# Attention gathered into the first batch's MoE, the other batches' MoE in two phases, and a fast product for two of them

## The chip, the cores and the metric

The kernel runs on one core of a Trainium2 chip. The core has a matmul engine (TensorE, PE in the rows), three engines for elementwise work (VectorE = DVE, ScalarE = ACT, GpSimd = POOL), and SyncE (SP), on whose queue this kernel issues all its transfers. PSUM is split into eight banks of 512 floats for each of 128 partitions; matmuls write there, and GpSimd does not read it. The metric is device time of one execution in microseconds (us). Three runs of the kernel before took 859.25, 853.92 and 858.77 us, median 858.77. The profile is that of one execution, with a span of 857.7 us from the first to the last instruction.

## What is computed

Four batches of attention (8 heads, 576 positions, 64 per head), then two feed-forward layers over all 2304 tokens. The attention of a head is the sum of two: a coarse one over means of four positions, repeated back to 576, and a local one in which a position sees only those less than four away.

```python
out_d = sm_attn(q_d, k_d, v_d)               # 144 x 144 per head
out_up = np.repeat(out_d, factor, axis=2)
mask = np.abs(pos[:, None] - pos[None, :]) < factor
...
x = (out_up + out_local).transpose(0, 2, 1, 3).reshape(B * S, H * D)   # 2304 x 512
h = x @ moe_w_in                             # 512 -> 2048
g = h * np.clip(h + 3.0, 0.0, 6.0) / 6.0
x = g @ moe_w_out                            # 2048 -> 512
h = np.maximum(np.maximum(x @ w1, x @ w2), x @ w3)   # 512 -> 768, three times
out = h @ moe2_w_out                         # 768 -> 512
```

q, k and v are float32; the weights of both layers arrive as float64, and the kernel makes float32 of them itself.

## The kernel before

**Products.** A float32 operand x is split into two float16 parts, hi and lo, scaled by a power of two, and a product is three float16 matmuls: hi hi, hi lo and lo hi. Each such matmul is one instruction of 128 x 128 weights on 288 (first MoE), 384 or 512 columns (second MoE). The scales come from `pow2_scale`, a chain of some ten small operations that begins with sums of squares.

**First MoE.** A batch has 576 tokens in two halves of 288. For each half and each of the 16 blocks f of 128 hidden units, `moe1_h` makes h in a bank (12 matmuls, L1052), ACT makes Relu of h (r, L1063), DVE the product with h (gf, L1067), ACT the hi part of g (L1070), DVE or POOL the lo part (L1072), and `moe1_y` multiplies g with the weights of `wo` into four accumulators y (12 matmuls, L1086). h and y alternate: the h of later blocks stands between an h and its y. Batch 0 goes through the weights in four quarters, as they arrive, and adds y to the sum of the quarters on DVE (L1113) or POOL (L1110); batches 1 to 3 keep the accumulators over all 16 blocks.

**Weights.** `quarter` loads a quarter of w_in and w_out as 64-bit words, `to_f32` makes float32 of them in four passes, two on POOL (L899, L902) and two on DVE (L905, L909: the last sets the sign), ACT sums squares (L949), and `split` in L1005 and L1007 makes hi and lo. The weights of the second layer are loaded and converted in the same way by `m2_load` and `m2_wo`, during batch 3's MoE and the first pass of MoE 2.

**Attention** of a batch: loads of k, q, v (`load`, tile stg) and of a second layout of v (`load_vw`, 8 transfers per half); `transposes` into kT and qT (L581, L593) with sums of four positions (qkd, L614); `local_scores` (L756) and its softmax `soft`; `down_scores` (L657), one unit (two heads, one half of the positions) at a time; `down_pT` (L700), `down_out` (L717), `local_out` (L822), which adds both into x (L834), and `x_split` (L491, L493) into the fp16 pair x16. Most of its tiles have one buffer per name, so a batch's attention follows the one before. Batch 0's attention comes first; that of batch b > 0 is spread over the MoE of batch b - 1 and the first part of its own MoE.

**Second MoE.** Three passes over 768 tokens. w1, w2 and w3 each multiply y by seven products of half-size blocks where eight would be needed (`m2_a`, L1417; sums of blocks stand for the eighth), DVE takes the maximum over the three, and `m2_out` multiplies with w_out (L1488). `y_ops` makes the seven token operands, `m2_w1` and `m2_w23` the seven weight operands.

**Order.** All this is given as operations with a cost and a priority to `Plan`, which lays them out on the engines by list scheduling when the kernel is built; `PARAMS` holds the priorities and some choices (which sums go to POOL, which masks to PE). The instruction streams are then fixed: each engine goes through its own in order. PSUM banks have tags: at 2 (attention, output), h 2, y 4. A tile's buffers are given out in the order of the operations, tag `at` in any order. Where PE would stand idle before 94 us of the plan's time, `warm_up` matmuls that compute nothing are put in.

## Time and profile before

| | |
|---|---|
| median of three runs | 858.77 us (853.92 to 859.25) |
| span of the profiled execution | 857.7 us, 20,891 instructions |
| PE busy | 806.4 us, 94% |
| DVE busy | 564.2 us, 66% |
| ACT busy | 408.4 us, 48% |
| POOL busy | 201.7 us, 24% |
| HBM read and written | 49.8 and 4.7 MB |

The profiled execution's span is 1.1 us below the median. Matmuls overlap, so PE's busy time counts the stretches in which any runs, and says nothing of how much each does. The granted clock of PE is given as a share of 2.4 GHz; its two levels are 1.2 and 2.4, and a value between is a mean over the stretch.

### The profile page before, as it was taken

What the parts mean: (1) busy time and instruction counts of PE and PEld (TensorE: products, weight loads), DVE (VectorE), ACT (ScalarE), POOL (GpSimd) and SP (SyncE); (2) the same over time, 40 slices, a digit from 0 to 9 for tenths busy, and PEclk for the clock granted to TensorE, in tenths of its full rate; (3) what the DMA queues carried; (4) which work ended last, traced back from release to release, by engine and by line L of the source; (5) the groups of instructions that cost most, each with busy time, mean ns of one, the idle gap of its engine ahead of it and who ended that gap; (6) DMA issues with size and microseconds to landing.
All of it is one profiled execution on the core that took longest, in us unless ns stands there. A gap on an engine that the chain in (4) does not pass through costs nothing.

```text
span 857.7 us, 20891 instructions
## 1 busy us (share of the span) xinstructions
PE 806.4 (94%) x8823; PEld 574.6 (67%) x8823; DVE 564.2 (66%) x1219; ACT 408.4 (48%) x883; POOL 201.7 (24%) x232
## 2 busy tenths in 40 slices
PE   7698988697999999999999999999997999999998
PEld 7576876474787777777777777776654456546653
DVE  2689788987657645477364797667999336913670
ACT  4435566467365543565354464558434332523131
POOL 3253334232223000000010646313740400100000
PEclk8858999998999999999999999999999999999999
DMA  8957255322314120132000233420020100010001
GB/s 206 166 170 159 88 112 141 103 74 57 67 29 112 39 59 10 27 95 58 2 2 2 76 111 92 113 79 1 27 72 26 62 13 1 1 74 1 1 2 73
DMA packets 72888, 55.87 MB, mean 65 GB/s; under 512 B 54874, under 2 KB 61786, under 8 KB 72794
## 3 DMA queue, kind: packets, MB, share of 16 engines
q1 hardware_dynamic: 72794, 54.53, 24.6%
q8 instruction: 69, 1.13, 0.5%
q14 instruction: 25, 0.20, 0.1%
HBM read 49.81 MB, written 4.72 MB: 64 GB/s over the span
## 4 chain that ended last, share of the span: by engine, by line
PE 79%; DVE 13%; ACT 4%; issue 3%; DMA 1%; ACTq 0%; DVEq 0%
PE y L1086 20%; PE h L1052 19%; PE y L1417 16%; PE at L1488 8%; PE h L1417 3%; PE at L822 3%; PE at L657 2%; PE at L581 1%; PE warm L1573 1%; PE at L717 1%; PE at L700 1%; PE at L756 1%; DMA wi<-in_k_dram 1%; ACT r L1063 1%; DVE gf L1067 1%
## 5 line engine op out<-in xcount | busy, mean ns | idle before, releaser
L1052 PE MATMUL h<-x,wi 128*128 128x288 f16 x1536 | 220.7, 290 | 8.3 <-DVE gf L1067 3.6
L1086 PE MATMUL y<-g,wo 128*128 128x288 f16 x1536 | 217.0, 288 | 2.8 <-ACT y L1101 2.8
L1052 PEld LDWEIGHTS <-wi 128*128 128x128 f16 x1536 | 147.2, 99 | 49.4 <-issue 6.6
L1086 PEld LDWEIGHTS <-wo 128*128 128x128 f16 x1536 | 147.4, 98 | 43.6 <-issue 6.1
L1417 PEld LDWEIGHTS <-m2ow 128*128 128x128 f16 x756 | 73.8, 98 | 52.3 <-issue 3.8
L1063 ACT ACTIVATE r<-h,sc 128x288 f32<-128x288 f32 x96 | 56.5, 588 | 84.6 <-PE h L1052 84.3
L1067 DVE SCALAR_TENSOR_TENSOR gf<-r,sc,h 128x288 f32<-128x288 f32 x96 | 48.9, 510 | 60.8 <-ACT r L1063 60.4
L1417 PE MATMUL y<-yb,m2ow 128*128 128x384 f16 x468 | 81.7, 326 | 2.9 <-DVE y L1428 2.6
L1070 ACT CAST g<-gf 128x288 f16<-128x288 f32 x128 | 54.9, 429 | 53.9 <-DVE gf L1067 52.8
L1072 DVE TENSOR_TENSOR g<-gf,g 128x288 f16<-128x288 f32 x108 | 58.6, 543 | 23.7 <-ACT g L1070 23.2
L1488 PE MATMUL at<-m2fw,hm 128*128 128x512 f16 x324 | 70.6, 379 | 0.0
L1432 ACT COPY p<-y 128x384 f32<-128x384 f32 x54 | 25.9, 480 | 73.1 <-PE y L1417 66.3
L1417 PEld LDWEIGHTS <-m2w 128*128 128x128 f16 x378 | 37.3, 99 | 29.6 <-issue 5.2
L1488 PEld LDWEIGHTS <-hm 128*128 128x128 f16 x324 | 31.7, 98 | 37.8
L1072 POOL TENSOR_TENSOR g<-gf,g 128x288 f16<-128x288 f32 x20 | 15.1, 757 | 171.7 <-ACT g L1070 118.1
L1428 DVE TENSOR_TENSOR u<-h,p 128x384 f32<-128x384 f32 x27 | 14.9, 553 | 50.3 <-PE h L1417 45.9
L1428 DVE TENSOR_TENSOR y<-y,u 128x384 f32<-128x384 f32 x54 | 28.2, 560 | 26.2 <-ACT p L1432 25.9
L1573 PEld LDWEIGHTS <-warm 128*128 128x128 f16 x341 | 35.6, 110 | 6.8 <-issue 2.7
L1417 PE MATMUL y<-yb,m2w 128*128 128x384 f16 x234 | 40.1, 326 | 0.0
L1498 ACT ACTIVATE y<-at,sc 128x512 f32<-128x512 f32 x18 | 12.3, 686 | 52.2 <-PE at L1488 52.2
L822 PEld LDWEIGHTS at<-pl,vw 32*64 32x64 f32 x1536 | 28.1, 143 | 8.9 <-issue 6.5
L822 PE MATMUL at<-pl,vw 32*64 32x24 f32 x1536 | 32.1, 221 | 1.0 <-issue 1.0
(225 smaller groups left out, 1249.9 us busy)
## 6 DMA issues: line engine op xcount, KB each, us to landing
raw<-in_moe_w_dram SPq DMA_DIRECT2D x24, 384.0 KB
y<-in_moe_w_in_dram SPq DMA_DIRECT2D x8, 1024.0 KB
y<-in_moe_w_out_dram SPq DMA_DIRECT2D x8, 1024.0 KB
vw<-in_v_dram SPq DMA_DIRECT2D x62, 96.0 KB
out_dram<-y SPq DMA_DIRECT2D x18, 256.0 KB
stg<-in_k_dram SPq DMA_DIRECT2D x12, 288.0 KB
stg<-in_q_dram SPq DMA_DIRECT2D x12, 288.0 KB
stg<-in_v_dram SPq DMA_DIRECT2D x12, 288.0 KB
```

Of the source, the lines that this page charges most:

```text
L822: nc.tensor.matmul(out=T[pts[cc]][64 * hl:64 * hl + 64, i * QB:i * QB + QB], lhsT=T[n(f"vw{half}")][32 * c:32 * c + 32, i, hl, :], rhs=T[n ...
L1052: nc.tensor.matmul(out=hp(), lhsT=T[wt][:, a, kk, fi * P:fi * P + P], rhs=T[x16][:, e, kk, :], start=(kk == 0 and (a, e) == (0, 0)), stop= ...
L1063: op("ACT", c_act(CH, 2), prio + LEAD, lambda: nc.scalar.activation(out=T[r_], in_=hp(), func=AF.Relu, scale=col(INVH + 4 * b + g), bias=c ...
L1067: op("DVE", c_dve(CH, 1 if b else 0), prio + LEAD, lambda: nc.vector.scalar_tensor_tensor(out=T[gf], in0=T[r_], scalar=col(SIX + g) if b e ...
L1070: op("ACT", c_act(CH, 0, False), prio + LEAD, lambda: nc.scalar.copy(out=T[g16][:, 0], in_=T[gf]), r=[gf], w=[(g16, 0)], new=[buf(g16, "ac ...
L1072: op("DVE", c_dve(CH), prio + LEAD, lambda e: e.tensor_tensor(out=T[g16][:, 1], in0=T[gf], in1=T[g16][:, 0], op=ALU.subtract), r=[gf, (g16 ...
L1086: nc.tensor.matmul(out=T[acc[d]][:, 0:CH], lhsT=T[wt][:, a, fi, d * P:d * P + P], rhs=T[g16][:, e], start=(first and (a, e) == (0, 0)), st ...
L1417: nc.tensor.matmul(out=b(to), lhsT=w_op(nm, o)[:, a, kt, fp * P:fp * P + P], rhs=T[f"yb{p}{y}"][:, e, kt, :], start=(first and kt == 0 and ...
L1428: op(eng, c_dve(C2) if eng == "DVE" else 0.1 + C2 * 0.0021, pr, lambda: e.tensor_tensor(out=out(), in0=a(), in1=c(), op=fn), r=r, w=w, new ...
L1432: op("ACT", c_act(C2), pr, lambda: nc.scalar.copy(out=out(), in_=a()) if scale is None else nc.scalar.activation(out=out(), in_=a(), func= ...
L1488: nc.tensor.matmul(out=T[po], lhsT=h_hl(p, fp, fi, t)[:, a, i * P:i * P + P], rhs=T["m2wo"][:, e, fi * 3 + fp, :], start=((fp, fi) == (0, ...
L1573: nc.tensor.matmul(out=T["tail"][:, CH:512], lhsT=warm[:, 0:P], rhs=warm[:, 0:512 - CH], start=True, stop=True)
```

## The change

1. **Attention.** The attention of batches 1 to 3 is planned within batch 0's MoE. Its result stays in float32 (tile xy, in the space of a later y), and `x_split` runs only for batch 0. The transposes of batch 0 take tag at (2 banks) for y (4). `down_scores` handles two units at once, so its small operations on dsm cover four columns for two; exp writes to SBUF, and the normalisation may go to DVE or POOL. The two small softmax operations on mx cover both head groups. The lists in `PARAMS` send more work from DVE elsewhere: 11 y sums on POOL for 7, 8 lower halves for 5, 6 sums of four for 4, and 5 masks on PE for 3.
2. **PSUM.** at 2, a2 2, h 2, y 2. Accumulators of the later batches, products of the first MoE and products of MoE 2 take a2 and y in turn (`next_bank`).
3. **Batch 0's MoE** makes y per quarter, half and block d with 12 matmuls of four h each, in one bank at a time, in place of four accumulators over the blocks.
4. **Later batches in two phases.** `moe1_a` first makes all g of a batch (8 groups p of 2 blocks by 2 halves, tile ga, 8 buffers), `moe1_b` then all y, one accumulator of 48 matmuls after the other. The elementwise work on g covers 576 columns where it can.
5. **Seven for eight.** For batches 2 and 3 (`fast`) a group makes h in 7 products of 6 matmuls for 8. The weight operands S1 to S4 are made once by `w_pair` from hi and lo of w_in during batch 1, the token operands by `x_ops`. Sums of products: three copies on ACT, three additions on DVE.
6. **Conversion** in three passes: an ACT Prelu (its slope for negative values sets the sign), one POOL pass, one DVE pass. The weights of MoE 2 are converted once by `m2_convert`, planned after batch 2's h, written to DRAM in float32 and loaded from there by `m2_load` and `m2_wo`; sums of blocks may go to DVE or POOL.
7. **Pools and plan.** Two more swaps of SBUF space (attn to str, act to act2) stand between batch 0 and the later batches. The plan has new priorities, allows any order for some banks, and counts a cost for the fetching of PE's instructions. Warm products end at 36 us of the plan for 94.

```diff
@@ PARAMS @@
- 'red_pool': ((0, 'k', 0), (1, 'q', 1), (2, 'k', 0), (2, 'k', 1)), ... 'fill': 94.45, ...
+ 'red_pool': ((0, 'k', 0), (1, 'q', 1), (2, 'k', 0), (2, 'k', 1), (2, 'q', 0), (0, 'k', 1)),
+ 'mask_pe': ((0, 1), (1, 1), (2, 1), (3, 0), (3, 1)),
+ 'fill': 36.3156,
+ 'win': (44.8252, 83.8248, 125.3487, 166.0319, 224.1886),
+ 'tn': (188.9889, 279.4849, 362.3186, 430.3845),
+ 'fast': (2, 3)}
...
@@ banks and buffers @@
-    BUFS = {"at": 2, "h": 2, "y": 4, "x16": 3, "r": 2, "g16": 4, "yt": 2, "gf": 2, "stg": 2, ...
+    BUFS = {"at": 2, "a2": 2, "h": 2, "y": 2, "x16": 2, "r": 2, "g16": 8, "yt": 2, "gf": 2, "stg": 3, "vw": 1,
+            ... "x7": 7, "z": 2, "zo": 2, "ga": 8, "r2": 2, "s2": 3}
+    def next_bank():
+        turn[0] += 1
+        return "a2" if turn[0] % 2 else "y"
...
@@ to_f32 @@
-        op("POOL", c_f32(n), prio, lambda: nc.gpsimd.tensor_scalar(
-            out=dst(), in0=words()[1].bitcast(F32), scalar1=2.0 ** -112, scalar2=1.0,
-            op0=ALU.mult, op1=ALU.mult), r=r, w=w)
+        op("ACT", c_act(n, 0, False), prio, lambda: nc.scalar.activation(
+            out=dst(), in_=words()[1].bitcast(F32), func=AF.Prelu, scale=2.0 ** -112, alpha=-(2.0 ** 32)), r=r, w=w)
...
-        op("DVE", c_dve(n), prio, lambda: nc.vector.scalar_tensor_tensor(
-            out=dst().bitcast(I32), in0=words()[1], scalar=-2147483648, in1=dst().bitcast(I32),
-            op0=ALU.bitwise_and, op1=ALU.bitwise_or), r=list(r) + list(w), w=w, port=True)
...
@@ moe1_a @@
+        k1, s1 = keep("X", 1, product("A11", "B11", "X", first=True))
+        pr = product("A12", "B21", "Y", first=True)
+        add(0, 0, ps_("Y"), s1, [bk("Y"), k1], pr, [buf(ga, "act2", "ga", [P, 2, S])])
+        k5, s5 = keep("Z", 5, product("S1", "T1", "Z", first=True))
+        k2, s2 = keep("X", 2, product("S2", "T2", "X"))
+        pr = product("S3", "T3", "X")
+        add(1, 1, ps_("X"), s5, [bk("X"), k5], pr)
+        pr = product("S4", "B22", "Z")
+        add(0, 1, ps_("Z"), s2, [bk("Z"), k2], pr)
+        pr4 = product("A22", "T4", "X")
+        hard(0, [(lambda: T[ga][:, 0], S, 0, [(ga, (0, 0)), (ga, (0, 1))], False)], pr)
+        hard(1, [(cs(1, 1), CH, CH, [(ga, (1, 1))], False), (ps_("X"), CH, 0, [bk("X")], True)], pr4)
...
@@ order of the stages @@
+    swap(("attn",), "str", "right")
+    swap(("act",), "act2", "left")
+    for b in range(1, B):
+        x_ops(b, TN[b] - G["xp"][b - 1], G["xps"])
+        if b == first:
+            for g in range(NQ):
+                for i in range(2):
+                    w_pair(g, i, G["sp"] + G["sps"] * (2 * g + i))
+        for p in range(8):
+            moe1_a(b, p, TN[b] + 7 * c_mm(CH, 6) * p)
+        if b == first:
+            m2_convert(lambda n: G["mp"] - 5 + G["mps"] * n, lambda n: G["mp"] + G["mps"] * n)
+        moe1_b(b, TN[b] + 56 * c_mm(CH, 6) + G["bo"])
...
```

In `keep` ACT copies a bank to SBUF, `add` is an addition on DVE from a bank and such a copy into ga, and `hard` makes g of it: ACT Relu, DVE product, ACT hi part, DVE or POOL lo part, over 576 columns for the first block and, for Relu and product of the second, twice over 288.

## Rows read from the trace of the kernel before

**Rows 1.** The page, part 1: busy us, share of the span, instructions.

```profile
PE 806.4 (94%) x8823; PEld 574.6 (67%) x8823; DVE 564.2 (66%) x1219; ACT 408.4 (48%) x883; POOL 201.7 (24%) x232
```

**Rows 2.** Busy us (count) by stage: length; PE, PEld, DVE, ACT, POOL; clock, DMA, GB/s.

```profile
0.00:62.00 62.00, 47.54 (x727) 39.52 (x727) 36.26 (x84) 27.18 (x63) 24.61 (x48) 0.75 0.78 174
62.00:235.00 173.00, 149.30 (x2085) 114.55 (x2086) 144.04 (x305) 97.00 (x209) 54.53 (x44) 0.93 0.41 104
235.00:363.00 128.00, 126.17 (x1791) 99.25 (x1789) 73.55 (x193) 66.71 (x174) 17.38 (x25) 1.00 0.20 44
363.00:490.00 127.00, 125.98 (x1956) 98.87 (x1954) 75.77 (x193) 63.19 (x150) 20.29 (x25) 1.00 0.17 40
490.00:590.00 100.00, 99.71 (x810) 78.97 (x809) 74.67 (x142) 56.66 (x113) 37.20 (x49) 1.00 0.30 88
590.00:663.00 73.00, 66.78 (x397) 39.08 (x396) 69.77 (x136) 39.44 (x69) 34.82 (x34) 0.98 0.11 37
...
687.00:747.00 60.00, 60.00 (x369) 35.92 (x368) 38.48 (x82) 22.34 (x45) 4.09 (x3) 1.00 0.02 5
```

**Rows 3.** Stage 235 to 363, products of h (L1052) alone.

```profile
235.00:363.00 128.00, 54.89 (x384) 35.97 (x384) 1.00 0.20 44
```

**Rows 4.** Chain of work that ended last: start us, us, what.

```profile
480.30 1.47 PE y L1086 x12
...
605.06 5.85 PE y L1417 x36
...
663.53 23.31 PE at L1488 x108
```

**Rows 5.** The same chain, two pieces of the first 70 us.

```profile
25.25 5.21 issue
...
65.90 2.08 DVE wi L1007 x3
```

**Rows 6.** DVE groups of 62 to 235, line L909: busy us, mean ns, idle before.

```profile
L909 DVE SCALAR_TENSOR_TENSOR wo<-y,wo 128x1024 int32<-128x1024 int32 (+1 forms) x6 | 7.6, 1269 | 0.0
...
L909 DVE SCALAR_TENSOR_TENSOR wi<-y,wi 128x1024 int32<-128x1024 int32 x4 | 6.2, 1553 | 0.0
...
L909 DVE SCALAR_TENSOR_TENSOR y<-y,y 128x1024 int32<-128x1024 int32 x4 | 4.9, 1224 | 0.1
```

**Rows 7.** Groups of instructions over the span: busy us, mean ns, idle before.

```profile
L1063 ACT ACTIVATE r<-h,sc 128x288 f32<-128x288 f32 x96 | 56.5, 588 | 84.6 <-PE h L1052 84.3
L1070 ACT CAST g<-gf 128x288 f16<-128x288 f32 x128 | 54.9, 429 | 53.9 <-DVE gf L1067 52.8 <-DVE dsm L678 0.6
...
L493 DVE SCALAR_TENSOR_TENSOR x<-x,sc,x 128x576 f16<-128x576 f32 x16 | 13.3, 834 | 4.1 <-ACT x L491 3.7
L834 DVE TENSOR_TENSOR x<-at,od 128x288 f32<-128x288 f32 x32 | 13.2, 448 | 11.2 <-PE at L822 11.1
...
L491 ACT ACTIVATE x<-x,sc 128x576 f16<-128x576 f32 x16 | 12.3, 770 | 11.1 <-DVE x L834 11.1
...
L675 DVE TENSOR_SCALAR dsm<-dsm 72x2 f32<-72x2 f32 x32 | 8.5, 267 | 13.1 <-ACT at L672 12.2 <-ACT y L672 0.6
```

**Rows 8.** The subtraction in g (L1072) alone, by stage.

```profile
62.00:235.00 173.00, 15.49 (x25) 4.90 (x6) 0.93 0.41 104
235.00:363.00 128.00, 13.76 (x27) 3.65 (x5) 1.00 0.20 44
```

**Rows 9.** The product in g (L1067) alone, stage 235 to 363.

```profile
235.00:363.00 128.00, 16.72 (x33) 1.00 0.20 44
```

**Rows 10.** Busy us in two of 43 stretches of 20 us.

```profile
40.00:60.00 20.00, 16.26 (x280) 12.85 (x277) 18.17 (x38) 6.64 (x16) 14.07 (x17) 0.62 0.59 144
...
180.00:200.00 20.00, 15.63 (x128) 11.68 (x125) 14.82 (x40) 14.35 (x37) 6.09 (x6) 0.96 0.20 65
```

**Rows 11.** DVE groups of 590 to 663, conversion passes.

```profile
L905 DVE SCALAR_TENSOR_TENSOR m2fw<-m2fw,raw 128x256 int32<-128x256 int32 x12 | 8.7, 731 | 0.0
...
L909 DVE SCALAR_TENSOR_TENSOR m2fw<-raw,m2fw 128x256 int32<-128x256 int32 x12 | 5.3, 449 | 0.0
```

More of the change, by code (lines that the diff above doesn't have):

```diff
@@ L82, in op, with fetch @@
         return i
+    def fetch(self, t, cost, n):
+        late, a = 0.0, self.count
+        self.count += n
+        for b in range((a // self.BLOCK + 1) * self.BLOCK, self.count + 1, self.BLOCK):
+            at = t + late + cost * (b - a) / n
+            late += max(0.0, self.fetched - at)
+            at = max(at, self.fetched)
+            self.fetched = at + next(f for until, f in self.FETCH if at < until)
+        return late
     def schedule(self, fill=None, fill_until=0.0):
@@ L880, in attention @@
                 bring_v()
-            for u in range(4):
-                down_scores(half, u, at(key("dn"), u))
+            for e in range(2):
+                down_scores(half, e, at(key("dn"), 2 * e))
             for u in range(4):
@@ new lines, in pe @@
+                    out=T[acc][:, 0:CH], lhsT=T[wt][:, a, i, d * P:d * P + P], rhs=T[gs[i]][:, e],
+                    start=(i == 0 and (a, e) == (0, 0)), stop=(i == FQ - 1 and (a, e) == (1, 0)))
+        for i in range(FQ):
+            op("PE", c_mm(CH, 3), prio + 0.01 * i, lambda i=i: pe(i), ni=6,
+               r=[(gs[i], 0), (gs[i], 1), (wt, (i, 0)), (wt, (i, 1))], w=[(acc, 0)],
+               new=[bank(acc, "y")] if i == 0 else [])
+        yt = lambda: T[ysb][:, d, half * CH:half * CH + CH]
@@ L1282, in m2_wo @@
[L1282 removed]
+            new = [buf("m2wo", "late", "m2fw3", [P, 2, NF2, DM], F16)] if i == 0 else []
+            vk = [("m2wof", i), ("sc", "m2o")]
             op("ACT", c_act(2 * DM, 1, False), p_split(i), lambda src=src, sl=sl: nc.scalar.activation(
@@ L1535, in swap_m2 @@
-    def swap_m2():
-        attn.release()
-        pools["m2"] = tc.alloc_tile_pool(name="m2", bufs=1, side="right")
-    def swap_late():
-        wts.release()
-        act.release()
-        cvp.release()
-        pools["late"] = tc.alloc_tile_pool(name="late", bufs=2)
-    w3, t2 = WIN[3], WIN[4] + 6
+    attention(0)
+    bring_quarter(0)
+    for g in range(NQ):
+        for half in range(2):
+            for i in range(FQ):
+                moe1_h(g, half, i, when(g, half, i))
+            for d in range(NK):
+                moe1_y(g, half, d, when(g, half, 3) + G["yo"] + G["yd"] * d)
+        if g + 1 < NQ:
+            bring_quarter(g + 1)
@@ new lines, with swap, go @@
+    for b in range(1, B):
+        attention(b)
+        x_consts(b, G[f"p{b}"]["q1"][0] - 2)
+    last = [set()]
+    def swap(old, name, side):
+        def go():
+            for o in old:
+                pools[o].release()
+            pools[name] = tc.alloc_tile_pool(name=name, bufs=1, side=side)
+        opened[name] = op("POOL", 0.0, -5.0, go, after=set().union(*last, *(used[o] for o in old)))
+        last[0] = {opened[name]}
+    swap(("attn",), "str", "right")
+    first = FAST[0]
+    swap(("act",), "act2", "left")
```

895 lines of the change are left out of this document (584 added, 311 removed), and 8 rows, old and new, of tables (PARAMS, PARTS).

## The prediction

> **What bounds the kernel now.** I read the page's busy shares first: TensorE (PE) is busy for 94% of the span [rows 1], which says only that it is the engine to follow. The busy times by stage come next, with the stages cut where the first and last products of each part fall [rows 2]. Batch 1's stage, 235 to 363 us, holds its 384 h products [rows 3] and as many y products. How long a product takes when nothing disturbs it stands in the chain of work [rows 4]: 12 of 288 columns in 1.47 us (0.1225 us each), 36 of 384 in 5.85 (0.1625), 108 of 512 in 23.31 (0.216). So one batch of the first MoE is 768 x 0.1225 = 94.1 us, the second MoE is three passes of 378 x 0.1625 + 23.31 = 84.7, together 254. Batch 1's stage is 128 us long with PE busy for 126, so one batch's attention occupies PE for 128 - 94 = 34 us, and nothing there is lost but 2 us.
>
> Against these numbers the stages show where time is lost. 0 to 62: attention of batch 0 in front of any h product. 62 to 235: 173 us for 94 of MoE and 34 of attention, 45 lost; VectorE (DVE) is busy 144 of 173, 83%, and the clock row says 0.93. 235 to 363 and 363 to 490: nearly nothing. 490 to 590: 100 us for 94.1, 6 lost. 590 to the end: 268 us for 254; since pass two, 687 to 771, is 84 long and pass three the same, all but a drain of some 2 us is lost in the first pass, where DVE is busy 69.8 of 73. So PE sets the end except in two stages where DVE does: batch 0's MoE and the first pass of MoE 2.
>
> **The change, stage by stage.** Sums go by the span of this execution, 857.7 us; it is 1.1 us below the median of the runs, 858.77, which I add at the end.
>
> *Start, 62 us.* The change takes one DVE and one POOL pass from each converted weight tile and puts one ACT pass there; it moves wi0's load behind all loads of batch 0's attention on SP, gives the transposes two PSUM banks (at) for four (y), and ends the warm products at 36 for 94. The chain before the first h ends in DVE passes over wi [rows 5], which speaks for a few us of gain; later loads and fewer banks speak for as much loss. I take 62, with 57 to 66.
>
> *Batch 0's MoE with the attention of batches 1 to 3.* PE's work: 94.1 + 3 x 34 = 196 us. DVE's: it had 144 us [rows 2]. Off go the last conversion pass (L909 at 7.6 + 6.2 + 4.9 = 18.7 us [rows 6]) and batch 1's split (4 x 0.834 = 3.3 [rows 7]). On come two more attentions. In batch 1's stage DVE is busy 73.6, of which gf is 16.7 and g 13.8 [rows 2, 8, 9]; 43 remain, less four maxima over y at about 0.75 (an estimate from the 576-element split, 0.834): 40, less the split that moves to later stages: 37, so 74 for two. Pairing the units in down_scores halves the count of three small operations, none longer than 0.267 [rows 7], 2.5 us a batch. Eleven y sums on POOL for seven, eight lower halves for five and two more masks on PE take some 8. DVE: 144 - 18.7 - 3.3 + 74 - 7.5 - 8 = 181. At its 83% that is 218 us. ACT: 97, plus two attentions at 66.7 - 32 x (0.588 + 0.429) - 8 y copies at 0.5 - splits of 3.1 = 27 [rows 2, 7], plus 14 new conversion passes at about 1.2 (0.429 for 288 elements and 0.770 for 576, carried on to 1024), less a split: 165, 75% of 220 where it was 56%. Three engines are then near full and each waits for the others, so I add 7: 225. Bounds: PE alone, 196; DVE at the 74% of 180 to 200 us [rows 10], 245.
>
> The single buffers of qT, kT and qkd put the three attentions behind one another; batch 0's took 62 us alone, so three fit in 225, and I cost that at nothing. Their loads go past the weight quarters on SP: 0.41 x 173 = 71 us of transfers now, and 0.20 x 128 = 26 more for each attention [rows 2], 123 of 225. The transfer engines are half full, so this too costs nothing as long as the stage is that long; below 196 both would show.
>
> *A rule that speaks against this stage.* DVE's subtraction in g took 15.49 / 25 = 0.620 us here, where POOL was busy 54.5 of 173, and 13.76 / 27 = 0.510 in batch 1's, where POOL was busy 17.4 of 128 [rows 2, 8]. The Trainium skill (SBUF — State Buffer, "SBUF: two separate sides") says that DVE and GpSimd hold a common port pair as an exclusive lock, so that one waits for the other's whole instruction. The trace agrees in direction: 0.11 us an operation, not a whole POOL instruction each time. POOL loses one conversion pass and gains attention, and stays near the same share, so the sum already holds this; were all 181 us stretched by that 0.11 in 0.51 again, the stage would be 39 us longer, 867 in all, which is past the range's far end.
>
> *Batch 1.* 768 products as before, 94.1 us. In front of it stand two pool swaps: x_ops needs the space of the last attention, ga that of batch 0's g. The first two splits (0.77 + 0.83 each) stand before the first product; 3 us: 97. DVE's S operands for seven products and ACT's copies lie beside these products.
>
> *Batches 2 and 3.* h: 8 groups of 7 x 6 products for 8 x 6, 336 for 384; y stays 384: 720 x 0.1225 = 88.2 us each, 5.9 less than before. But the group of 42 products (5.15 us) now has, on DVE, three additions at 0.448, one product over 576 at 0.834, two over 288 at 0.510 and two subtractions over 576 between 0.85 and 1.09: 4.9 to 5.4 us; one subtraction may go to POOL, 4.0 to 4.3. On ACT: three copies at about 0.4, two Relu at 0.588, one of 576 at 0.77, two casts at 0.65 to 0.86: about 4.6 [rows 7]. Both are near 90% of PE's 5.15. At the 83% of batch 0's stage, 4.6 / 0.83 = 5.5, 0.4 over, 16 groups: 6 us. Bounds: 0 (in 235 to 490 nothing was lost) and 16 (DVE with nothing on POOL, 5.15 / 0.83 = 6.2). The y half has almost no elementwise work and covers MoE 2's weight conversion, which moves there with 36 loads, 36 stores to DRAM and 15 reloads on SP; behind a store waiting for its conversion stand only the next raw loads. Cost nothing.
>
> *MoE 2.* 268 before. DVE loses the conversions of w_out in pass one, 8.7 + 5.3 = 14.0 us [rows 11], against a loss of 12. It keeps the splits of w2, w3 and w_out and may take POOL's subtractions. 56 of 61.4 us is still 91%, so I leave 5 of the 12: 261 (254 to 268).
>
> Sum: 62 + 225 + 97 + 2 x 88.2 + 6 + 261 = 827, and 1 for the median: **828 us**.
>
> **Rivals.** (a) *The clock falls in batch 0's stage*, the slower side. Half of PE's work there becomes small products. From 40 to 60 us PE was busy 16.3 of 20 with such work and the granted clock was 0.62 [rows 10]; the whole of 0 to 62 has 0.75, half of the time at 1.2 GHz. At 0.75 the 196 us become 196 / 0.75 = 261, with the stage's usual 5% of waits 274, and the sum is 876. It decides from a stage of 225 + 30 = 255 on. Against it: 235 to 490 keeps 1.00 with a quarter of PE's time in attention, and 62 to 235 has 0.93 while DVE holds PE up. By the Trainium skill (TensorE: Matmul & The Clock Gate, "What's actually happening") the throttled state is the default and activity lifts it; the rows at 40 to 60 us agree.
>
> (b) *The h groups of batches 2 and 3 go by DVE and ACT.* Then seven products save nothing: 5.88 us a group as before, or 6.2, is 12 to 17 us over, and batch 1's h, whose DVE also makes S (eight pairs of one sum and four small results, each then split: about 35 us by the rows' 0.45 to 1.1), loses some 10 more: 840 to 852. For it speak the 4.6 to 5.4 us against 5.15; against it the idle y halves and six banks that let two groups overlap. This is also the case in which the change does not do what it says.
>
> (c) *Everything packs.* Batch 0's stage runs as PE alone, 200, MoE 2 loses 2, the groups nothing: 62 + 200 + 96 + 176 + 257 + 1 = 792, up to 811 with half of it. For it speaks that 235 to 490 was packed with the same kinds of work at DVE 58%; against it that DVE would have to reach 90%.
>
> (d) *Instructions come late.* At 25.25 us PE stands for 5.21 us in the middle of a run of small score products with nothing that it waits for [rows 5]. Three attentions with one such gap each are 16 us in batch 0's stage, 843; in 235 to 490, with two attentions, PE is busy for 252 of 255 us [rows 2], so it is in the range only.
>
> **How the numbers follow.** Forecast, 812 to 846: 0.45. (c), 790 to 811: 0.20. (b) and (d), 846 to 861: 0.17. (a), above 861: 0.14. Under 790: 0.04. The range 796 to 864 leaves about 0.07 below and 0.12 above. One measurement of this kernel tells about 1% from no change: faster means below 850, slower above 867. Faster: 0.45 + 0.20 + 0.04 and a third of (b), 0.75. Same: the rest of (b) and a little of (a), 0.13. Slower: 0.12.
>
> **What would show it.** First h at 57 to 66 us; batch 1's first h, which marks the end of batch 0's stage, at 280 to 295; DVE there at 80 to 85% and the clock above 0.9; batches 2 and 3 at 88 to 96 us each with 336 h products; h groups nearer 5.2 than 5.9 us; MoE 2 under 264. A clock under 0.8 in batch 0's stage, or h groups above 5.8 us, would make the prediction wrong; a stage of 205 us with DVE above 88% would make it wrong the other way.

## The result, and the profile after

The changed kernel takes 820.03 us (median of four runs, 813.09 to 823.33), the kernel before 859.01 (853.92 to 861.21) on the same chip. The ratio is 0.9554, with a 95% interval of 0.9495 to 0.9613: 39 us, or 4.5%, faster. The forecast was 828.0, with 796 to 864.

The profiled execution has a span of 821.5 us, the longest of the four (811.3, 815.1 and 821.4 are the others). First the page of the changed kernel, part 1 (busy us, share of the span, instructions), to be laid beside [rows 1].

```profile
PE 778.4 (95%) x8518; PEld 552.9 (67%) x8518; DVE 556.5 (68%) x1157; ACT 452.5 (55%) x993; POOL 146.8 (18%) x185
```

PE's share is 95% where it was 94%, and that hides everything: what changed is where PE works and how much it has to do. The stages show it. They are cut at the first h product of batch 0 and of batch 1, at the start and the end of the h halves of batches 2 and 3, and at the first product of MoE 2; columns as in [rows 2]. A few products lie on the other side of a cut: batch 2's first 18 stand at 340.8 us, within batch 1's stretch.

```profile
0.00:68.70 68.70, 51.37 (x961) 43.87 (x962) 36.99 (x100) 37.23 (x98) 23.06 (x50) 0.73 0.79 158
68.70:285.00 216.30, 196.12 (x3882) 148.10 (x3879) 172.85 (x415) 148.56 (x357) 74.19 (x78) 0.89 0.53 125
285.00:384.90 99.90, 98.94 (x787) 77.93 (x788) 67.37 (x122) 47.91 (x92) 7.50 (x5) 0.97 0.00 1
384.90:426.10 41.20, 40.96 (x333) 32.32 (x332) 37.81 (x69) 37.88 (x84) 10.43 (x14) 1.00 0.32 80
426.10:473.10 47.00, 47.00 (x386) 37.49 (x384) 21.14 (x35) 25.03 (x60) 9.07 (x15) 1.00 0.68 190
473.10:514.30 41.20, 41.20 (x336) 32.58 (x334) 35.23 (x76) 36.98 (x88) 6.83 (x11) 1.00 0.39 112
514.30:561.00 46.70, 46.70 (x383) 37.22 (x382) 32.02 (x53) 24.48 (x49) 2.53 (x5) 1.00 0.27 83
```

The reader sees batch 0's stage at 216 us with three attentions in it, batches 2 and 3 at 41.2 + 47.0 and 41.2 + 46.7 us with PE idle for 0.2 us in all, and a DVE that is busy for 37.8 of 41.2 us in an h half and holds PE up for no more than that.

The kernel before has its first h at 67.0 us (not at 62, where the prediction cut), and the last product of its batch 3 ends at 590. So the 36.2 us between the two spans split like this:

| stretch | before | after | difference |
|---|---|---|---|
| start, to the first h | 67.0 | 68.7 | +1.7 |
| first MoE, four batches, with the attentions | 523 | 492.4 | -30.6 |
| MoE 2, to the end | 267.7 | 260.4 | -7.3 |

In the kernel before, six products of MoE 2 stand ahead of batch 3's last twelve, from 587.4 us on; cut there, the last two differences are 28.0 and 9.9. So MoE 2 gains 7 to 10 us and the first MoE 28 to 31, by where one cuts. From the table alone one can't say whose the 30 us are: seven products for eight, the attention gathered in one place, the conversion pass, or the fewer warm products. The experiments are about the first three, and about MoE 2's share.

Where PE still stands in batch 0's stage, the waits of PE from 68 to 286 us tell (engine, operation and line, what it waits for; us in total, times, longest):

```profile
PE y L1252 <- ACT y L1263: 5.2, 1, 5.2
PE a L914 <- issue: 2.5, 1, 2.5
PE h L1215 <- DVE wi L1176: 2.3, 3, 1.0
PE h L1215 <- issue: 2.2, 1, 2.2
PE a L1427 <- ACT x L655: 1.7, 1, 1.7
```

One wait of 5.2 us is the largest: at 112 us a y product needs a bank that ACT (L1263) has yet to copy out, and with two y banks for four that copy is due at once; ACT has other operations in front of it. No wait comes more than three times, and all idle time of PE is 20.2 of 216 us (216.30 - 196.12).

### The profile page after: what moved, and what is told of

Same layout as the page of the kernel before. It is cut to its first block, busy times and chain, and to the rows that moved or that the text cites. A ratio compares the mean times of both kernels' runs of the same rounds, so it can differ in the third digit from the quotient of the medians.

```text
span 821.5 us, 20337 instructions
## 1 busy us (share of the span) xinstructions
PE 778.4 (95%) x8518; PEld 552.9 (67%) x8518; DVE 556.5 (68%) x1157; ACT 452.5 (55%) x993; POOL 146.8 (18%) x185
## 4 chain that ended last, share of the span: by engine, by line
PE 61%; DVE 2%; ACT 2%; issue 1%; POOL 0%; DVEq 0%; ACTq 0%
PE y L1468 17%; PE a L1765 9%; PE y L1765 9%; PE at L1836 9%; PE a L1377 5%; PE h L1765 3%; PE a L1427 2%; PE y L1427 2%; PE y L1377 2%; PE h L1427 2%; PE h L1377 1%; ACT r L1402 0%; DVE hm L1776 0%; ACT ga L1411 0%; PE at L987 0%
## 5 line engine op out<-in xcount | busy, mean ns | idle before, releaser
L1468 PE MATMUL y<-ga,wo 128*128 128x288 f16 x1152 | 142.6, 286 | 0.0
L1215 PE MATMUL h<-x,wi 128*128 128x288 f16 x384 | 65.1, 315 | 6.5 <-DVE wi L1176 2.3
L1252 PE MATMUL y<-g,wo 128*128 128x288 f16 x384 | 59.7, 298 | 5.3 <-ACT y L1263 5.2
L1215 PEld LDWEIGHTS <-wi 128*128 128x128 f16 x384 | 38.1, 105 | 20.6 <-issue 5.2
L1427 PEld LDWEIGHTS <-wi 128*128 128x128 f16 x384 | 38.5, 100 | 13.8 <-ACT x L655 1.8
L1413 DVE TENSOR_TENSOR ga<-r,ga 128x576 f16<-128x576 f32 x48 | 37.7, 786 | 12.2 <-ACT ga L1411 11.5
L1377 PEld LDWEIGHTS <-S 128*128 128x128 f16 x384 | 37.6, 98 | 9.5
L1765 PE MATMUL a<-yb,m2ow 128*128 128x384 f16 x234 | 42.9, 326 | 0.3 <-DVE a L1776 0.3
L1765 PE MATMUL y<-yb,m2ow 128*128 128x384 f16 x234 | 43.1, 326 | 0.0
L1411 ACT CAST ga<-r 128x576 f16<-128x576 f32 x48 | 32.1, 671 | 10.4 <-DVE r L1406 10.2
L1377 PEld LDWEIGHTS <-wi 128*128 128x128 f16 x288 | 28.0, 98 | 7.8 <-issue 0.6
L837 ACT ACTIVATE pd<-a,dsm 72x144 f32<-72x144 f32 x64 | 23.3, 372 | 17.0 <-DVE dsm L831 17.0
```

The source lines that it names most:

```text
L837: op("ACT", c_act(SD, 2) + 0.09, prio, lambda i=i, j=j, x=x: nc.scalar.activation(out=T[pds[j]][:, i], in_=view(j)[:, i], func=AF.Exp, bia ...
L1215: nc.tensor.matmul(out=hp(), lhsT=T[wt][:, a, kk, i * P:i * P + P], rhs=T[x16][:, e, kk, :], start=(kk == 0 and (a, e) == (0, 0)), stop=(k ...
L1252: nc.tensor.matmul(out=T[acc][:, 0:CH], lhsT=T[wt][:, a, i, d * P:d * P + P], rhs=T[gs[i]][:, e], start=(i == 0 and (a, e) == (0, 0)), sto ...
L1377: nc.tensor.matmul(out=ps_(x)(), lhsT=lhs(a, kt), rhs=T[xn][:, e, kt, :], start=(first and kt == 0 and (a, e) == (0, 0)), stop=(kt == 1 an ...
L1411: op("ACT", c_act(S, 0, False), pr, lambda: nc.scalar.copy(out=hl(0), in_=T[r_]), r=keys, w=[(ga, (fb, 0)), (ga, (fb, 1)), (ga, (fb, "hi") ...
L1413: op("DVE", c_dve(S), pr, lambda e: e.tensor_tensor(out=hl(1), in0=T[r_], in1=hl(0), op=ALU.subtract), r=keys + [(ga, (fb, "hi"))], w=[(ga ...
```

## The experiments

Two theories of the 30 us. *Theory 1*: PE sets the h halves of batches 2 and 3, so seven products for eight are worth what 96 fewer products take (11.8 us), and the rest comes from batch 0's stage, where three attentions fill what used to be idle. *Its rival*: DVE and ACT set the h halves, and the gain is that DVE lost a conversion pass. Beside these stands theory C of the expectations: up to some 140 us DVE's passes over the arriving weights set the pace of either kernel, and behind it PE does. Two further questions: what the low clock between 40 and 140 us costs (0.68 there, theory A in the expectations), and what gave MoE 2 its 7 to 10 us.

The changed kernel's 820.03 us were taken once, and the runs below on four chips. The kernel before, run beside each of them, had medians of 857.26 to 859.30, so a difference of 2 us to 820.03 says nothing.

### Four runs in which the plan was made again

These four change one thing in the source and let the list scheduling lay out everything anew.

**Eight products for batches 2 and 3.**

```diff
-        if b not in FAST:
+        if True:
```

> One part undone: batches 2 and 3 of the changed kernel make h in eight products per group (48 matmuls) as batch 1 does, with four token operands for seven. The weight operands S are still made, as work that nothing reads, so that VectorE's load in batch 1's stage stays. Theory 1 (the matmul engine sets these stages; their h groups go at 42 x 0.1225 = 5.15 us): each of the two batches takes 94.1 us for 88.2, the kernel 820 + 11.8 = 832 us, and the h half of a batch goes from 41.2 to 47.1 us. Rival (VectorE and ScalarE set the pace of the h groups, so the eighth product was hidden): batches at 88 to 90 us, kernel 820 to 823.

Measured: 860.25 us (854.04 to 866.56, ten runs), ratio to before 1.0024 (0.9977 to 1.0071). From batch 1's first h to MoE 2 it takes 290.6 us for 276.1, 14.5 more, near the 11.8 of theory 1. But another 24 us are lost in MoE 2, which this edit doesn't touch. The waits of PE from 560 to 700 us:

```profile
PE y L1765 <- ACT m2w L1578: 14.4, 1, 14.4
PE y L1765 <- DVE m2w L1580: 3.7, 1, 3.7
PE a L1765 <- DVE m2w L1580: 2.7, 1, 2.7
```

The new plan put the splits of w1 late, since its priorities were chosen for another set of operations. The total of this run says nothing of seven for eight.

**Warm products to 150 us of the plan.**

```diff
- 'fill': 36.3156,
+ 'fill': 150.0,
```

> The changed kernel with matmuls that compute nothing put into the idle time of the matmul engine up to 150 us of the plan's time, where it ends at 36 (and at 94 in the kernel before). Theory A (the low clock between 60 and 140 us, 0.50 to 0.84 in the profile of the changed kernel, holds the engine up): the granted clock there rises above 0.9, the stage from the first h to batch 1's first h falls from 216 us by 10 to 25, the kernel to 797 to 812 us. Theory B (VectorE sets that stage, the matmul engine waits for it at either clock): the clock rises, the stage stays within 4 us of 216, the kernel within 815 to 825.

Measured: 852.11 us (848.01 to 857.15, ten runs). The clock did rise where it was meant to, and fell elsewhere (columns as in [rows 2]):

```profile
80.00:120.00 40.00, 35.61 (x523) 29.72 (x521) 31.48 (x70) 31.13 (x72) 12.83 (x12) 0.99 0.73 174
200.00:280.00 80.00, 73.38 (x1106) 52.34 (x1104) 56.10 (x164) 44.84 (x122) 13.29 (x17) 0.66 0.26 64
```

Batch 1's first h comes at 310.7 us for 285.0. The order of the stage is another, so the run doesn't tell what the clock at 80 to 120 is worth.

**wi0's load first on SP.** One priority, -78.55 to -680.

> The changed kernel with the load of the first quarter of w_in placed directly behind the two loads of k of batch 0, where it stood behind all loads of batch 0's attention. Theory 1 (this load, issued at 32.6 us, makes the first h late at 68.7 us; it was at 62 to 64 before): the first h starts at 60 to 64 us and the kernel takes 813 to 817 us. Rival (the start is set by the attention of batch 0, whose small products run at a clock of 0.5 to 0.7): the first h stays at 67 to 70 us, the kernel at 818 to 823; with the other attention loads pushed back it may get later.

Measured: 840.65 us (839.48 to 848.62); first h at 74.9 us, later than 68.7, batch 1's first h at 303.1. The load came earlier and the first h didn't: no support for the load as the cause, and again a new order. Before, the first h was at 67.0 us and not at the 62 to 64 that the expectation names.

**Four conversion passes,** the two on POOL and the sign pass on DVE as before.

> One part undone: the changed kernel with the conversion of weights in four passes as in the kernel before (two on GpSimd, two on VectorE, none on ScalarE). Theory B (VectorE sets batch 0's stage): it gets some 18.7 us more work there, the stage grows by 15 to 25 us and the first h comes 2 to 4 us later, the kernel 838 to 850 us; the conversions of MoE 2's weights lie in the y halves and cost nothing. Theory A (clock and the matmul engine's own work set it): the stage grows by under 8 us, the kernel 820 to 829.

Measured: 871.61 us (870.38 to 875.37); first h at 87.9, batch 1's first h at 309.3, MoE 2 at 594.5. More than either theory expected (838 to 850 at most), and so mixed with a new order.

What follows from the four together: each made the kernel 20 to 52 us slower than the changed kernel, whatever was edited, with losses also in stages that the edit doesn't touch (MoE 2 in the first run). With a planner, "undo one part" undoes the fit of the priorities as well. In the runs below the plan is that of the kernel tested, and an edit adds, removes or shortens instructions inside an operation that has its place already, or shifts a few operations behind a named one. Two of these runs change nothing ahead of batch 1's first h (the eighth product, and the one on MoE 2's first pass); they have it at 283.6 and 283.0 us, where the changed kernel's profile has 285.0. A shift of this mark by 2 us is therefore no effect.

### Seven runs with the order kept

**The eighth product back, in its place.** The last of the seven products of a group (A22 by T4) is issued twice.

```diff
-                for kt in range(2):
+                for kt in range(4 if last else 2):
...
-        pr4 = product("A22", "T4", "X")
+        pr4 = product("A22", "T4", "X", last=True)
```

> The changed kernel with the order of every engine kept: only the last product of each of the 16 seven-product groups (A22 by T4) is issued twice, 12 matmuls for 6, so h of one block of tokens holds that product twice. Theory 1 (the matmul engine sets the h halves of batches 2 and 3): each of the two h halves goes from 41.2 to 47.1 us, the kernel from 820 to 832 us. Rival (VectorE and ScalarE set them): h halves at 42 to 44, the kernel 821 to 825.

Measured: 829.98 us (825.85 to 833.38), ratio 0.9661. From batch 2's first h to MoE 2, first this kernel, then the changed one:

```profile
338.60:569.90 231.30, 231.30 (x1888) 184.42 (x1886) 159.79 (x296) 141.37 (x317) 31.29 (x48) 1.00 0.32 90
```
```profile
340.80:561.10 220.30, 220.06 (x1791) 174.92 (x1790) 159.04 (x296) 139.51 (x317) 34.57 (x48) 1.00 0.34 94
```

96 products more make the stretch 11.0 us longer, with the same work on DVE and ACT and PE busy throughout. 96 x 0.1225 is 11.8. So PE sets these halves, theory 1 holds for them, and the rival "by DVE and ACT" falls.

**Warm products behind the small ones, 36 to 110 us of the plan.** 72 more products that compute nothing, each behind a small one.

> The changed kernel with the order of every engine kept; between 36 and 110 us of the plan's time 72 matmuls that compute nothing (224 columns) are put behind the small products of attention. They cost 0.1 us each at the full clock, 7 us, and 0.2 at half, 14. Theory A (the low clock holds up batch 0's stage): the granted clock between 40 and 140 us rises from 0.66 to above 0.85, batch 1's first h comes 5 to 20 us earlier than 285, the kernel takes 800 to 815 us. Theory B (VectorE holds it up): the clock may rise, batch 1's first h stays at 281 to 290, the kernel at 816 to 826.

Measured: 832.44 us (832.00 to 834.39). The stretch from 40 to 140 us, this kernel and then the changed one:

```profile
40.00:140.00 100.00, 86.49 (x1434) 62.97 (x1432) 74.30 (x174) 66.36 (x147) 27.84 (x33) 0.69 0.60 162
```
```profile
40.00:140.00 100.00, 81.33 (x1426) 60.63 (x1424) 77.74 (x183) 70.93 (x156) 30.48 (x33) 0.68 0.74 174
```

The clock stayed (0.69 for 0.68) and batch 1's first h came 10.2 us later, at 295.2. The experiment missed its aim: it did not raise the clock, and so doesn't price it. Both theories' ranges were missed. It does show that 72 products put behind small ones cost 12 us of the median, though PE is idle for 18.7 of these 100 us in the changed kernel.

**The fourth pass back on DVE, in its place.**

```diff
...
+            nc.vector.scalar_tensor_tensor(
+                out=dst().bitcast(I32), in0=words()[1], scalar=-2147483648, in1=dst().bitcast(I32),
+                op0=ALU.bitwise_and, op1=ALU.bitwise_or)
...
```

> The changed kernel with the order kept; VectorE's pass that sets the sign follows each of its conversion passes, as a second instruction in the same place (the sign is there already, so the result is the same). That is 8 x 0.55 + 12 x 1.25 = 19 us more VectorE work before batch 1's first h and 36 x 0.5 = 18 us in the y halves of batches 1 to 3. Theory B (VectorE sets batch 0's stage): batch 1's first h comes 14 to 22 us later, the kernel takes 834 to 844. Theory A (clock and small products set it): under 8 us later, the kernel 820 to 828. In the y halves both theories expect nothing.

Measured: 841.89 us (840.28 to 842.20). Batch 0's stage of this kernel:

```profile
66.70:297.40 230.70, 201.61 (x3881) 150.21 (x3877) 191.25 (x430) 149.84 (x357) 74.24 (x78) 0.86 0.48 117
```

DVE has 191.25 us of work for 172.85, and the stage is 230.7 us for 216.3: 14.4 of the 18.4 us come out at the end, though DVE's share is 83%. This is theory B's range. Of the 14.4 us, 8.9 are more idle time of PE and 5.5 more busy time, at a mean clock of 0.86 for 0.89, so part of the delay was paid at the low clock.

Where the delay arises can be read by following a product by its number, since the order is the same. The 250th product of 128 x 288 starts 82.1 us behind the first h in the changed kernel (at 150.8 us) and 95.2 us behind it here: 13.1 of the 14.4 us are lost by then. Eleven of the added passes (12.7 us of DVE) stand between these two products; the four behind (6.8 us) cost 1.3 us more.

From batch 1's first h to MoE 2 the kernel takes 282.6 us for 276.1, 6.5 more, where nothing was expected: in the h halves of batches 2 and 3 PE now waits for s from ACT (2.5 us in all) and for ga and r from DVE (1.8), which it did for 0.2 us before the edit:

```profile
PE a L1383 <- ACT s L1398: 1.9, 1, 1.9
PE a L1383 <- DVE ga L1393: 1.4, 3, 0.8
```

The weights of MoE 2 are converted there, and DVE had little room.

**Less softmax work in batches 1 to 3.** The local softmax there covers 1 of 12 blocks, which leaves out most of it (with the masks on PE, the subtraction keeps all 12).

```diff
-            mx = n(f"mx{half}")
+            mx, m = n(f"mx{half}"), 12 if b == 0 else 1
...
-                dve(D_, lambda: nc.vector.tensor_reduce(out=T[mx][:, 0, hl], in_=raw(), axis=AX.X, op=ALU.max),
+                dve(D_, lambda: nc.vector.tensor_reduce(out=T[mx][:, 0, hl, 0:m], in_=raw()[:, 0:m], axis=AX.X, op=ALU.max),
```

> The changed kernel with the order kept; for batches 1 to 3 the local softmax's maximum, its subtraction, its sum and its normalisation cover one block of 24 queries for twelve (the rest is left out), which takes 12 x some 1.7 = 20 us from VectorE and GpSimd in batch 0's stage and nothing from the matmul engine. Theory B (VectorE sets the stage, busy 173 of 216 us): batch 1's first h comes 13 to 20 us earlier, the kernel takes 800 to 808. Theory A: under 6 us earlier, the kernel 814 to 821.

Measured: 817.79 us (815.60 to 818.81), ratio 0.9527. The second part of batch 0's stage, this kernel and the changed one:

```profile
140.00:281.50 141.50, 134.42 (x2956) 105.48 (x2955) 103.59 (x288) 92.61 (x243) 48.85 (x60) 0.97 0.40 92
```
```profile
140.00:285.00 145.00, 136.54 (x2972) 105.90 (x2970) 114.68 (x291) 93.86 (x247) 52.23 (x60) 0.97 0.39 94
```

DVE's time in the whole stage falls by 15.0 us (172.85 to 157.81), 11 of them here. The part is 3.5 us shorter, and 2 of these lie within what the mark moves without an edit. From 140 us on PE is busy for 94 to 95% of the time in either kernel. Theory A's range was met: DVE doesn't set this part. That agrees with the run before, where passes up to some 150 us, while the weights arrive, cost their full time and later ones hardly any.

**The kernel before without its fourth pass.** L909 left out, so the weights have no sign; the order is that of before.

```diff
-        op("DVE", c_dve(n), prio, lambda: nc.vector.scalar_tensor_tensor(
-            out=dst().bitcast(I32), in0=words()[1], scalar=-2147483648, in1=dst().bitcast(I32),
-            op0=ALU.bitwise_and, op1=ALU.bitwise_or), r=list(r) + list(w), w=w, port=True)
+        op("DVE", c_dve(n), prio, lambda: None, r=list(r) + list(w), w=w, port=True)
```

> The kernel before with its order kept and the last conversion pass (L909 on VectorE, which sets the sign) left out, so that all weights count as positive. It takes 24 us from VectorE up to the end of batch 0's MoE and 20 us from batch 3's MoE and MoE 2's first pass. Theory B (VectorE sets batch 0's stage from end to end): batch 1's h starts 16 to 22 us earlier and MoE 2's first pass is 4 to 6 us shorter, the kernel 831 to 839 us for 859. Theory C (VectorE and the conversions set only the first part of that stage, up to about 140 us, and the matmul engine's own work the rest; so a gain is the part that falls ahead of 140 and shrinks to two thirds): 8 to 14 us there, the kernel 840 to 849.

Measured: 851.88 us (846.90 to 853.12, seven runs), ratio 0.9917 (0.9886 to 0.9948): 7 us by the medians, 13 by the two profiled executions. In the profile the first h stands at 59.9 us for 67.0. First this kernel's start, then that of before:

```profile
0.00:59.90 59.90, 46.61 (x755) 39.12 (x755) 33.95 (x91) 29.60 (x68) 24.61 (x48) 0.85 0.88 200
```
```profile
0.00:67.00 67.00, 52.26 (x756) 43.18 (x757) 40.43 (x97) 29.74 (x69) 24.61 (x48) 0.73 0.81 180
```

The same products took PE 5.7 us less there, at a clock of 0.85 for 0.73; only 1.4 us of the 7.1 are less waiting. So how much of the earlier start is the pass, and how much the clock of that one execution, is not shown. The stretch behind it, again this kernel first:

```profile
67.00:140.00 73.00, 68.28 (x942) 55.35 (x941) 51.25 (x109) 43.35 (x95) 22.43 (x21) 0.98 0.44 129
```
```profile
67.00:140.00 73.00, 63.09 (x882) 50.18 (x881) 62.18 (x116) 39.66 (x90) 26.68 (x20) 0.96 0.48 120
```

60 more PE products stand in the same 73 us, but this kernel is 7 us further on there; counted by products, the first 300 of 128 x 288 take 73.1 us for 75.4, 2.3 us less. Batch 1's h is some 11 us earlier in this profile, which is theory C's 8 to 14 and not B's 16 to 22; the median, 851.88, misses C's 840 to 849 too. The first pass of MoE 2 shortens by 2.6 us. Taking the pass out of the kernel before is thus worth 7 us by the medians, against 22 that putting it into the changed kernel costs. The changed kernel's first h, at 68.7, is no earlier than before's.

**wo0's raw words in buffers of their own,** so that their load doesn't wait on SP.

```diff
+                    if g == 0 and nm == "wo":
+                        new = [(new[0][0], lambda raw=raw, j=j: T.__setitem__(raw, yp.tile(
+                            [P, 2, 512], I64, tag=("y1", "y0")[j], bufs=1, name=("y1", "y0")[j])))]
```

> The changed kernel with the order kept; the two raw tiles of the first quarter of w_out lie in buffers of their own (the tags y1 and y0, free by then) and do not wait for those of w_in. In the changed kernel SP stands 14.1 us at this load, from 44 to 58 us, and batch 1's loads of k, q and the next weights stand behind it. Theory 1 (these loads feed batch 0's first quarter, and the stage up to 140 us goes by when its weights arrive): the load is issued at about 44 us, batch 1's first h comes 4 to 12 us earlier than 285, the kernel takes 808 to 816. Rival (the order of conversions on VectorE and ScalarE is fixed and late anyway): batch 1's first h at 282 to 287, the kernel 817 to 823.

Measured: 822.61 us (816.10 to 825.24). The load is issued at 44.6 us for 58, the 14 us for which SP stood are gone, and batch 1's first h is at 286.6 for 285.0. The rival's ranges were met: the stalled queue cost nothing that this run can see. A likely reason, not tested, is that with every engine's order fixed, what waits for that load is placed after other work anyway.

**The first y copies on ACT earlier.** The eight copies of the first quarter are placed right behind their products.

> The changed kernel; alone the eight ScalarE copies that empty the y banks of the first quarter are placed directly behind their products in ScalarE's order, 0 to 8 us of the plan's time earlier, ahead of softmax and square operations that wait for VectorE. Theory 1 (with two y banks for four, the matmul engine waits for this copy: 5.2 us at 112 us in the changed kernel): that wait goes, batch 1's first h comes 3 to 6 us earlier, the kernel takes 814 to 817. Rival (the wait hides another one, for g or for scores, directly behind it): batch 1's first h at 283 to 287, the kernel 818 to 822.

Measured: 821.35 us (814.35 to 823.10, six runs), ratio 0.9545 (0.9508 to 0.9582). Two waits of PE from 68 to 286 us (lines of this run's kernel, 13 further down):

```profile
PE at L632 <- ACT qT L764: 3.4, 1, 3.4
...
PE y L1265 <- ACT y L1276: 1.2, 1, 1.2
```

The wait for the y copy falls from 5.2 us to 1.2, and one of 3.4 us for another ACT operation (qT) stands in the list. Batch 1's first h is at 281.7 us, 1.3 to 3.3 us earlier than without this edit; the medians don't differ. The wait was mostly replaced.

### One run on MoE 2's first pass

DVE makes the lower half of each of the 14 operands of w2 and w3 twice: as much added work as the two conversion passes of w_out that left this pass [rows 11].

```diff
-        op("DVE", c_dve(KH * FH, 1), prio, lambda: nc.vector.scalar_tensor_tensor(
+        def low():
+            for _ in range(times):
+                nc.vector.scalar_tensor_tensor(
...
-            split_op(lambda: w_op(nm, o), src, col(S_W2), p, [key, ("sc", "m2")], [wop_key(nm, o)], new)
+            split_op(lambda: w_op(nm, o), src, col(S_W2), p, [key, ("sc", "m2")], [wop_key(nm, o)], new, times=2)
```

> The changed kernel with the order of every engine kept, but DVE makes the lower half of each of the 14 weight operands of w2 and w3 twice: 14 more operations of 1.0 to 1.2 us, 15 us more on DVE, all in the first pass of MoE 2, about the 14 us that the two conversion passes of w_out took there in the kernel before; the result is the same. If these 14 us set the 7 us that MoE 2 lost before and no longer loses, the first pass becomes 4 to 9 us longer (DVE 73.6 + 15 = 88.6 of 88 us), with waits of PE for DVE's maxima, and the median is 824 to 829. If MoE 2's 7 us came from something else (ACT, the order of the maxima, the loads), the pass grows by less than 2 us and the median stays at 819 to 822. Both theories expect nothing before MoE 2.

Measured: 832.56 us (827.50 to 837.66), ratio 0.9708. The stretch from MoE 2's first product to its first output product, this kernel, the changed one and before:

```profile
558.20:632.40 74.20, 62.22 (x374) 36.20 (x372) 71.22 (x124) 34.15 (x56) 5.63 (x3) 1.00 0.18 64
```
```profile
561.10:622.10 61.00, 60.69 (x375) 36.38 (x373) 57.29 (x110) 34.00 (x56) 5.64 (x3) 1.00 0.22 78
```
```profile
587.40:663.40 76.00, 69.49 (x416) 40.75 (x414) 72.53 (x140) 41.00 (x71) 34.82 (x34) 0.98 0.10 35
```

and PE's waits there, which in the changed kernel come to 0.3 us:

```profile
PE a L1768 <- DVE a L1779: 5.9, 3, 2.5
PE y L1768 <- DVE y L1779: 3.5, 2, 1.7
PE y L1768 <- DVE hm L1779: 1.9, 3, 0.8
```

The pass is 13.2 us longer, more than the 4 to 9 expected, and nearly all of the 13.9 us (71.22 - 57.29) that DVE got more. The direction is settled, and a reason for the size is at hand: the changed kernel's DVE is busy for 57.3 of 61.0 us, so there were 3.7 us of room, where the expectation went by 73.6 of 88 us, a longer stretch. The conversions' leaving is enough to account for all that MoE 2 gained. That it is the only cause is not shown: POOL's work in this stretch also fell, from 34.8 us to 5.6.

## Why the prediction was right, point by point

| term | predicted | measured | why |
|---|---|---|---|
| start | 62 (57 to 66) | 68.7 | the mark was misread: before's first h is at 67.0 |
| batch 0's stage | 225 (196 to 245) | 216.3 | below |
| batch 1 | 97 | 99.9 | 2.2 of it are batch 2's first 18 products; the clock is 0.97 |
| batches 2 and 3 | 176.4 + 6 | 88.2 + 88.0 | h halves lose nothing |
| MoE 2 | 261 (254 to 268) | 260.4 | the sum met, the 5 us left in lie elsewhere |

The sum was 827 for a span of 821.5. It is near because misses cancel in part: 6.7 us too little at the start and 2.9 in batch 1's stretch, 8.7 + 6 too much in batch 0's stage and the h halves. That much of the hit is luck.

*The start.* The step that failed is a reading. The prediction cut before's stages at 62 us and took this for the first h, which is at 67.0. The chain of work there still ends in DVE passes over wi at 65.90 us [rows 5]. In the sum before's next stage was cut at the same 62, so the error moved 5 us from one term to the other. The sign (first h at 57 to 66) failed. Of "gain of a few, loss of as much" neither is priced by a run: the earlier start of the kernel before without its pass may be mostly the clock of that execution. What the changed kernel does ahead of its first h also differs: some 270 more products of attention (384 score products kT, qT for 192) and 69 fewer warm ones. Loads behind the attention's on SP and two banks for four weren't separated; the load alone didn't do it in the run with wi0 early, but that run had another order.

*Batch 0's stage.* The sum was made on DVE: 181 us at 83%. DVE has 172.9 us at 79.9%, 216, just under the sign of 80 to 85%. The forecast of DVE's work and share was good, and its cause was half right. DVE does set the part up to some 150 us (the fourth pass put back costs 13.1 us up to there and 1.3 behind); from then on PE sets it (11 us less on DVE give 1.5 to 3.5). Two terms on PE were missed that cancel. The attention was priced at 34 us, what was left of 128 us beside 94; PE's busy 126.2 leaves 32. From 140 to 285 us PE does 569 products of 128 x 288, 69.7 us at 0.1225, and 2403 small ones in the other 66.8 of its 136.5 busy us, 0.028 us each; the stage has 3114 small ones, 87 us and not 102. Against this stands the clock: from 68.7 to 140 us PE is busy for 59.6 us with 201 large products and 711 small ones, 44.4 us by the same prices, so some 15 us (an estimate from these counts) are the half clock's. That the 196 us forecast for PE met its 196.1 is luck.

*The clock, rival (a).* The sign "clock above 0.9" failed: 0.89 of 2.4 GHz as a mean of the two levels. Three of the windows of 20 us show where.

```profile
60.00:80.00 20.00, 18.78 (x357) 14.79 (x354) 16.83 (x41) 14.47 (x29) 5.74 (x6) 0.50 1.09 248
...
120.00:140.00 20.00, 18.72 (x297) 12.59 (x297) 16.60 (x36) 17.44 (x31) 8.54 (x7) 0.56 0.75 189
140.00:160.00 20.00, 20.00 (x347) 15.91 (x345) 12.84 (x34) 15.85 (x47) 8.13 (x12) 1.00 0.54 147
```

So the mechanism of (a) was there, for 71 of 216 us and not for all, and at about a third of its price (15 us for 274 - 225 = 49). The 357 products from 60 to 80 us, with PE busy for 94%, had a granted clock of 0.50, half speed throughout; the 347 from 140 to 160 us had 1.00. The Trainium skill (TensorE: Matmul & The Clock Gate, "What's actually happening") calls the throttled state the default that activity releases. The rows neither confirm nor deny it: the prediction took those of 40 to 60 us as agreeing, but PE was busy for 81% of them at 0.62, and the run with 72 more products kept 0.69. Which work releases it is not settled here.

The nearest to a price of the clock on record are the four executions of the changed kernel: 821.5 and 821.4 us at a mean clock of 0.943, 815.1 at 0.949, 811.3 at 0.954. Time and clock go together, by 10 us in these four, but this doesn't show which is the cause.

*Rival (b), h groups by DVE and ACT.* It had "4.6 to 5.4 us against 5.15" for it, and falls by the eighth product: 11.0 us of 11.8. DVE at 37.8 of 41.2 us and ACT at 37.9 held PE up for 0.2 us. The step that was mis-sized is "at the 83% of batch 0's stage, 6 us": a share reached amid waits of three engines for each other isn't the most that DVE can do. In this loop, which repeats the same group, 92% passed. The fourth pass put back shows that this was close to the limit: 6.5 us lost.

*Rival (c), everything packs,* came true for batches 2 and 3 and for MoE 2's first pass (PE busy for 60.69 of 61.00 us), and not for batch 0's stage (216 for 200) or MoE 2 as a whole (260.4 for 257), which is why the time lies between (c) and the forecast. *Rival (d), late instructions:* gaps "issue" of 2.5 and 2.2 us, where it was 5.21 before [rows 5]; in the range only, as said.

*MoE 2.* The mechanism holds by the last run: 14 us put back cost 13. The 5 us left in for the first pass weren't spent there, PE was idle for 0.3 us; PE stands 4.1 us in the last 89.5 us instead, which the sum had at 2. So 261 for 260.4 is in part luck.

*A rule that speaks against this stage.* The subtraction in g (L1235) takes 0.554 us in batch 0's stage, with POOL busy for 74.2 of 216 us:

```profile
L1235 DVE TENSOR_TENSOR g<-gf,g 128x288 f16<-128x288 f32 x24 | 13.1, 554 | 6.6 <-ACT g L1233 6.5
```

Before it took 0.620 with POOL busy for 54.5 of 173, and 0.510 with 17.4 of 128 [rows 2, 8]. By the exclusive lock of the Trainium skill (SBUF — State Buffer, "SBUF: two separate sides"), by which one waits for the other's whole instruction, I would expect the stretch to follow POOL's share. Against batch 1's 0.510 the direction agrees, the size doesn't: 34% of POOL goes with 0.044 us and 32% went with 0.11. No run here took POOL's work away alone.

*What the gain is made of,* then: 11 us by seven products for eight (shown by the eighth put back), 7 to 10 in MoE 2, for which the conversions that left are enough (a put-back of equal size costs 13), and some 17 to 20 in batch 0's stage and the attention. For these only parts are shown: the fourth pass costs 14 us in this stage when it is put back, and gave 7 in all when it was taken from the kernel before.

That gathering the attention gives the rest was argued and not tried. PE's time ahead of MoE 2 (590 us before, 561 after) fits it: idle time falls from 41.3 to 38.7 us and the time of warm products from 45.7 (341 of them) to 21.0 (144), so together by 27, while all other work takes 501 us for 503. The warm products in whole, before in two groups (L1573), then after (L1935):

```profile
L1573 PE MATMUL warm<-warm 128*128 128x224 f16 x213 | 31.7, 314 | 1.1 <-POOL warm L1576 1.1
...
L1573 PE MATMUL h<-warm 128*128 128x224 f16 x128 | 13.9, 259 | 2.0 <-ACT r L1063 1.3 <-DVE gf L1067 0.6
```
```profile
L1935 PE MATMUL warm<-warm 128*128 128x224 f16 x144 | 21.0, 312 | 1.1 <-POOL warm L1938 1.1
```

The 11 us that seven products save there seem to be lost again to the lower clock, if the estimate above holds. But the same figures leave a rival that no run tested: 197 fewer warm products may be a gain by themselves, since 72 added ones cost 12 us. The warm products alone, left out of the kernel before with its order kept, would tell.

## What to carry to other kernels

Where a planner lays out the code, test a part with the order frozen; the four runs planned anew were 20 to 52 us slower, as much as the effects looked for or more. Before adding work to an engine or taking it away, read its share in the stage and not in the span: DVE at 94% of MoE 2's first pass charged 13 of 14 us, DVE at 79% from 140 to 285 us gave back at most 3.5 of 11. Look also at how much of PE's busy time is warm products, which the share counts as work. And a share that one stage reached under mutual waits need not be the ceiling of a regular loop elsewhere: here 80% and 92%.

## What the runs showed of the hardware

Not expected: streams of small products keep PE busy for 94% of 20 us at a granted clock of 0.50 (60 to 80 us of the changed kernel), so a full PE row can hide half speed; with 72 added products the mean of 40 to 140 us was 0.69 for 0.68. A queue that stood 14 us (SP at wo0's load) gained nothing that shows when it was set free (822.61 us for 820.03). And PE stood 2.5 us in the middle of small products with nothing that the profile shows it waited for.
